# Four weight matrices of a three-stage kernel read three bytes on and decoded with one shift

## The chip, the cores and the metric

The kernel runs on one NeuronCore of a Trainium2 chip. The metric is the device time of one execution in microseconds (us): the median over several runs. The engines are called TensorE (PE), VectorE (DVE), ScalarE (ACT), GpSimd (POOL) and SyncE (SP) below. SP only issues DMAs here; POOL issues DMAs too.

## The reference

Three stages follow one another. The weights come as float64, and the kernel gets their raw 8 bytes as int64; all other inputs are float32.

```python
def _attn_ref(q, k, v, a_re, a_im):              # B, H, S, D = 4, 8, 768, 48
    mag = np.sqrt(a_re * a_re + a_im * a_im)
    scale = np.minimum(mag, 0.999) / (mag + 1e-06)
    a_re_n, a_im_n = (a_re * scale, a_im * scale)
    for t in range(S):                           # complex decay of a D x D state, per head
        new_re = ar * S_re - ai * S_im
        new_im = ar * S_im + ai * S_re
        S_re, S_im = (new_re + kv, new_im)       # kv: outer product of k[t] and v[t]
        y[:, :, t] = np.einsum('bhd,bhde->bhe', q[:, :, t], S_re)

def _moe_ref(x, w1, w2, w3, w_out):              # 384 -> 1024 -> 1024 -> 384
    a = x @ w1
    b = x @ w2
    h = a * b @ w3
    return h @ w_out

def _moe2_ref(x, w_in, w_out):                   # 384 -> 2048 -> 384
    h = x @ w_in
    sp = np.where(h > 20.0, h, np.log1p(np.exp(np.minimum(h, 20.0))))
    return (h * np.tanh(sp)) @ w_out
```

The output of one stage is the `x` of the next; there are 3072 tokens.

## The kernel before

The attention runs in two streams. `bh_stream(g)` (L190) computes, for each of three groups of steps and in blocks of 7 steps, the normalised decays and their running products: a chain of small DVE instructions (`steps`, L292 and L293, one pair per step; the scan L270; the products `scaled`, L310 and L313), fed by ACT (`squares`, `norm`: L215 to L246) and by POOL's loads `an` and `kqt`. The products go to DRAM (`kq_d`, stored by POOL's queue), and a small table ends each group (`table`, L327 to L332). `ch_stream` (L371) reads them back in 24 chunks (`tm`, SP's queue) and does the attention on TensorE: transposes (L421), state updates (L429), scores (L464), outputs (L477, L482). It can start a group only when that group's table is there (`ready`, L405).

The first dense stage is `m1_stream(i)` (L556), six tiles of 512 tokens, in three-product float32r arithmetic: each factor is split into a high and a low part (`split`, L132: an ACT copy and a DVE subtraction), and each product is three matmuls (`mm3`, L544). `w3 @ w_out` is folded into one matrix first by `fold_stream` (L167): three blocks of `w_out` and eight of `w3`, 128 x 1024 elements each, are loaded, decoded to float32 and multiplied (L180); the halves of the result stay in SBUF (`woh`, `wol`) and are also stored to `w3o_d` in DRAM (L183) for a fallback path. `w12(j)` (L551) loads and decodes two blocks of 128 x 384 for `w1` and `w2`, for j = 0 to 7, ahead of the first tile's matmuls. The second dense stage is the loop at L744 over 96 steps of (tile, f): `hid` (nine matmuls, L691), `soft` and `mish` (the activation), `fin` (nine matmuls, L718). Its weights `win` and `wout` are decoded before and in its first 27 steps.

`decode` (L138) turns the int64 words of a float64 into a float32: ACT scales the high word as a float (L149), which also sums its size into `wsum` for a range check; a second ACT instruction extracts three bits of the word (L160); DVE puts the sign in (L161) and joins the parts by a shift to the left (L164). For the `w3` blocks j = 2, 4 and 6 the sign goes another way (`signs=True`): ACT does four instructions (L149, L156, L157, L158) and DVE one (L164).

```python
A.activation(out=f, in_=top.bitcast(F32), func=AF.Abs, scale=W_SCALE, accum_out=...)   # L149
A.activation(out=low, in_=raw.bitcast(U16)[:, :, 1], func=AF.Relu, ...)                # L160
V.scalar_tensor_tensor(out=low, in0=top, scalar=-0x80000000, in1=low, ...)             # L161
V.scalar_tensor_tensor(out=t, in0=t, scalar=3, in1=low, op0=ALU.logical_shift_left, ...)  # L164
```

The raw words of `w1`, `w2`, `win` and `wout` share the tag `raw64`, which has two buffers. `in_range` (L726) turns the sums and flags into one number that decides at the end whether a general path, written for inputs out of range, runs (L766); it is called in step n = 40 of the last loop.

The order of the stages is written with `_merge` (L51): the fold with `bh_stream(0)`; then eight chunks of attention, `bh_stream(1)` and the first dense stage; then the same with `bh_stream(2)`; then what is left of the attention and the first dense stage with `win`; then the last loop. Within that, a scheduler of the tile framework places the instructions of each engine at build time, so an instruction may stand far ahead of its place in the text; what runs on an engine then runs in that fixed order.

Of the kernel before, what the change touches and what calls it, by code (L numbers as in the profile page):

```python
# [13 lines left out]
I32 = mybir.dt.int32  # L14
AF = mybir.ActivationFunctionType
# [5 lines left out]
HD = H * D  # L21
# [14 lines left out]

W_SCALE = 2.0 ** -112
# [28 lines left out]
def kernel(  # L66
# [33 lines left out]
    flags = const.tile([128, sum(n_blk) + 1], F32, name="flags")  # L100
    wsum = const.tile([128, 64], F32, name="wsum")
    cb = const.tile([128, 7], F32, name="cb")
# [6 lines left out]
    w3o_d = dram.tile([128, 2, 8, HD], F32, name="w3o_d")  # L109
# [28 lines left out]
    def decode(src, n, dst=None, raw=None, pool=None, cap=False, signs=False):  # L138

        if raw is None:  # L140
            raw = (pool or stg).tile([128, n, 2], I32, tag="raw64", name="raw64")
        nc.sync.dma_start(out=raw.rearrange("p n z -> p (n z)"), in_=src.bitcast(I32))
        t = dst if dst is not None else stg.tile([128, n], I32, tag="dec", name="dec")
        f = t.bitcast(F32)
        i = n_flags[0]
        if not cap:
            n_flags[0] += 1
        low, top = raw[:, :, 0], raw[:, :, 1]
        A.activation(  # L149
            out=f, in_=top.bitcast(F32), func=AF.Abs, scale=W_SCALE, accum_out=None if cap else wsum[:, i:i + 1]  # L150
        )
        if cap:
            V.tensor_scalar(out=f, in0=f, scalar1=W_MAX, scalar2=None, op0=ALU.min)
        if signs:
            r16 = raw.bitcast(U16)
            A.activation(out=r16[:, :, 0], in_=r16[:, :, 1], func=AF.Relu, scale=2.0 ** -13, bias=cb[:, 3:4])  # L156
            A.activation(out=top.bitcast(F32), in_=top.bitcast(F32), func=AF.Sign, bias=cb[:, 4:5])  # L157
            A.activation(out=raw.bitcast(I16)[:, :, 1], in_=top.bitcast(F32), func=AF.Identity, scale=16384.0, bias=cb[:, 5:6])  # L158
        else:
            A.activation(out=low, in_=raw.bitcast(U16)[:, :, 1], func=AF.Relu, scale=2.0 ** -13, bias=cb[:, 3:4])  # L160
            V.scalar_tensor_tensor(  # L161
                out=low, in0=top, scalar=-0x80000000, in1=low, op0=ALU.bitwise_and, op1=ALU.bitwise_or
            )
        V.scalar_tensor_tensor(out=t, in0=t, scalar=3, in1=low, op0=ALU.logical_shift_left, op1=ALU.bitwise_or)  # L164
        return f

    def fold_stream():  # L167
# [3 lines left out]
        for c in range(3):  # L171
            decode(wo[:, c], 1024, wos[:, c * 1024:(c + 1) * 1024], bufs[c][0])
            yield 2.0
        wos = wos.bitcast(F32).rearrange("p (k n) -> p k n", k=8)
        for j in range(8):
            raw, dst = bufs[j % 3]
            f = decode(w3t[:, j], 1024, dst, raw, signs=j in (2, 4, 6)).rearrange("p (k m) -> p k m", k=8)
# [4 lines left out]
            for z, w in enumerate((woh, wol)):  # L182
                nc.sync.dma_start(out=w3o_d[:, z, j], in_=w[:, j].bitcast(F32))  # L183
# [367 lines left out]
    def w12(j):  # L551
        for src, n in ((w1, "w1"), (w2, "w2")):
            f = decode(src[:, j], 3 * 128)
# [79 lines left out]
    V.memset(cb[:, 6:7], -0.4995)  # L633

# [44 lines left out]

    hw, hbs, gg, accs = {}, {}, {}, {}  # L680
# [44 lines left out]

    def in_range():  # L726
# [17 lines left out]
    for n in range(len(seq) + LAG2):  # L744
# [14 lines left out]
        if n == 40:  # L759
# [6 lines left out]
    with tc.If(ok < 1):  # L766
        general_path(tc, af, kqf, vf, w1, w2, win, wout, w3o_d, perm, gsum, out, decode)


def general_path(tc, af, kqf, vf, w1, w2, win, wout, w3o_d, perm, gsum, out, decode):  # L770
# [6 lines left out]
    with ExitStack() as st:  # L777
# [57 lines left out]
        with tc.tile_pool(name="g_b", bufs=1) as p, tc.tile_pool(name="g_ps2", bufs=1, space=PSUM) as pp:  # L835
# [8 lines left out]
            w3p = p.tile([128, 2, 8, HD], F32, name="w3p")  # L844
            nc.sync.dma_start(out=w3p, in_=w3o_d)
            w3o = p.tile([128, 8, HD], F32, name="w3o")
            V.tensor_tensor(out=w3o, in0=w3p[:, 0], in1=w3p[:, 1], op=add)
# [150 lines left out]
```

## Time and profile before

| | before |
|---|---|
| median of 3 runs | 1077.1 us |
| lowest and highest run | 1075.57 and 1080.53 us |
| span of the profiled execution, first to last instruction | 1079.1 us |
| TensorE busy | 935.3 us (87%) |
| VectorE busy | 702.2 us (65%) |
| ScalarE busy | 691.0 us (64%) |
| GpSimd busy | 108.9 us (10%) |
| mean granted TensorE clock | 0.944 of full speed |
| moved by DMA | 124.36 MB |

The execution that was profiled gives a span; no separate time of its own is listed for it. Its span lies 2.0 us above the median of the runs and between the lowest and the highest of them. A busy time is summed over the whole span; the stages have different limits, so the views that are cut by time are of more use. Two neighbouring instructions of one engine overlap in their records by some 0.1 us, so a cost on an engine is better taken from one start to the next.

### The profile page before, as it was taken

The page shows a single profiled execution, that of the slowest core. Times are in us where ns is not written, and L with a number is a line of the kernel's source. Part 1 is how long each engine was busy: PE and PEld are TensorE (multiplying, and loading weights), DVE is VectorE, ACT ScalarE, POOL GpSimd, SP SyncE. Part 2 cuts the span into 40 slices and gives each one's busy share as a digit, 9 for nine tenths or more (in the row PEclk, how much of TensorE's full clock was granted, in tenths as well). Part 3 has the DMA queues.
Part 4 walks back from the last instruction along what each step waited for, and adds up shares of the span by engine and source line. Part 5 has one row for each costly group of instructions (what it writes and reads, how often), then busy time and mean ns, then how long its engine had stood idle before and what let it go on. Part 6 is the DMA issues. An engine that isn't in the chain of part 4 may idle for free.

```text
span 1079.1 us, 13826 instructions
## 1 busy us (share of the span) xinstructions
PE 935.3 (87%) x4952; PEld 754.5 (70%) x4952; DVE 702.2 (65%) x1334; ACT 691.0 (64%) x1263; POOL 108.9 (10%) x161
## 2 busy tenths in 40 slices
PE   0586006879999999999999999999999999999997
PEld 0243005758788778888888888888888888887876
DVE  5989797899898999462335522688565644645552
ACT  6987466877787686574445422998656665466672
POOL 1212242222212222000000000000000000000000
PEclk9988556889999999999999999999999999999999
DMA  8675559995786875664533300122100101000000
GB/s 304 218 242 149 155 149 249 225 248 131 199 226 163 208 219 115 160 189 115 128 64 127 87 30 29 59 89 59 59 1 10 50 1 59 1 19 10 1 30 33
DMA packets 72509, 124.36 MB, mean 115 GB/s; under 512 B 7574, under 2 KB 45776, under 8 KB 71024
## 3 DMA queue, kind: packets, MB, share of 16 engines
q1 hardware_dynamic: 60880, 85.41, 28.4%
q0 software_dynamic: 11552, 37.98, 13.5%
q8 instruction: 41, 0.67, 0.3%
q14 instruction: 36, 0.29, 0.1%
HBM read 84.16 MB, written 36.18 MB: 112 GB/s over the span
## 4 chain that ended last, share of the span: by engine, by line
PE 62%; DVE 7%; DMA 3%; ACT 2%; issue 1%; SPq 0%; DVEq 0%; ACTq 0%
PE ps_h L549 18%; PE ps_o L549 17%; PE acc L549 7%; PE pa L549 7%; PE pb L549 6%; PE ps_a L464 2%; PE ps_tr L421 2%; DMA ws<-w 1%; PE ps_u L429 1%; PE ps_y L477 1%; PE ps_y L482 1%; DVE t L292 1%; DVE kt L313 1%; DVE p L293 1%; DMA out<-osb 1%
## 5 line engine op out<-in xcount | busy, mean ns | idle before, releaser
L549 PE MATMUL ps_o<-gh,wuh 128*128 128x512 f32 x288 | 113.4, 395 | 2.0 <-ACT osb L722 1.7
L549 PE MATMUL ps_o<-gl,wuh 128*128 128x512 f32 x288 | 113.3, 393 | 0.4 <-DVE gl L134 0.4
L549 PE MATMUL ps_h<-x2h,wil 128*128 128x512 f32 x288 | 113.4, 394 | 0.0
L549 PE MATMUL ps_h<-x2h,wih 128*128 128x512 f32 x288 | 113.2, 393 | 0.0
L549 PE MATMUL ps_o<-gh,wul 128*128 128x512 f32 x288 | 112.8, 392 | 0.0
L549 PE MATMUL ps_h<-x2l,wih 128*128 128x512 f32 x288 | 112.1, 389 | 0.0
L134 DVE TENSOR_TENSOR gl<-hb,gh 128x1024 fp32r<-128x1024 f32 x48 | 58.6, 1223 | 76.2 <-ACT gh L133 76.2
L692 ACT ACTIVATE wb<-ps_h 128x512 f32<-128x512 f32 x96 | 56.1, 598 | 67.9 <-PE ps_h L549 67.7
L693 DVE COPY hb<-ps_h 128x512 f32<-128x512 f32 x96 | 64.7, 687 | 49.1 <-ACT wb L692 47.2
L571 DVE TENSOR_TENSOR u<-u,pb 128x512 f32<-128x512 f32 x48 | 32.8, 684 | 69.5 <-PE pb L549 69.3
L421 PE MATMUL ps_tr<-id_sb,tm 128*96 128x128 f32 x384 | 55.6, 288 | 25.1 <-DMA tm<-kq_d 22.5
L133 ACT CAST gh<-hb 128x1024 fp32r<-128x1024 f32 x48 | 50.2, 1048 | 35.0 <-PE ps_o L549 35.0
L421 PEld LDWEIGHTS ps_tr<-id_sb,tm 128*96 128x96 f32 x384 | 44.5, 132 | 35.5 <-issue 24.3
L292 DVE TENSOR_TENSOR t<-an,p 128x192 f32<-128x192 f32 x192 | 67.4, 351 | 0.7
L133 ACT CAST uh<-u 128x512 fp32r<-128x512 f32 x48 | 29.7, 618 | 59.6 <-DVE u L571 59.4
L180 PE MATMUL ps_f<-fw1h,fw1l 128*128 128x384 f32 x48 | 24.8, 692 | 48.7 <-DVE fw1l L164 48.7
L549 PEld LDWEIGHTS ps_o<-gh,wuh 128*128 128x128 f32 x288 | 54.0, 188 | 16.8 <-ACT osb L722 4.2
L549 PEld LDWEIGHTS ps_o<-gl,wuh 128*128 128x128 f32 x288 | 54.1, 188 | 12.7 <-DVE gl L134 1.1
L549 PEld LDWEIGHTS ps_h<-x2l,wih 128*128 128x128 f32 x288 | 54.1, 188 | 12.5
L549 PEld LDWEIGHTS ps_h<-x2h,wil 128*128 128x128 f32 x288 | 54.0, 188 | 12.5
L549 PEld LDWEIGHTS ps_o<-gh,wul 128*128 128x128 f32 x288 | 54.2, 188 | 12.0
L549 PEld LDWEIGHTS ps_h<-x2h,wih 128*128 128x128 f32 x288 | 54.1, 188 | 11.3
(177 smaller groups left out, 2402.3 us busy)
## 6 DMA issues: line engine op xcount, KB each, us to landing
tm<-kq_d SPq DMA_DIRECT2D x48, 384.0 KB, 5.9
an<-in_a POOLq DMA_DIRECT2D x27, 336.0 KB, 5.0
kqt<-in_kq POOLq DMA_DIRECT2D x27, 336.0 KB, 6.6
kq_d<-kt POOLq DMA_DIRECT2D x27, 336.0 KB, 3.9
kq_d<-kt POOLq DMA_DIRECT2D x54, 168.0 KB, 5.2
vv<-in_v SPq DMA_DIRECT2D x24, 256.0 KB, 2.8
raw<-in_w SPq DMA_DIRECT2D x16, 384.0 KB, 5.5
raw<-in_win SPq DMA_DIRECT2D x16, 384.0 KB, 4.2
```

The source lines that it names most:

```text
L133: A.copy(out=hi, in_=raw)
L134: V.tensor_tensor(out=lo, in0=raw, in1=hi.bitcast(F32), op=sub)
L180: T.matmul(ps, lhsT=f[:, kk], rhs=wos[:, kk], start=(kk == 0), stop=(kk == 7))
L292: V.tensor_tensor(out=t, in0=win2, in1=_bc(pv[:, ::-1], 2, 2), op=mul)
L293: V.tensor_tensor(out=p[:, j], in0=t[:, 0], in1=t[:, 1], op=add)
L313: V.tensor_tensor(out=kt, in0=_bc(kqt, 3, 2), in1=_bc(p[:, 0:m], 2, 2), op=mul)
L421: T.transpose(ps[:, hh], tm[n][:, h0 + hh, z], id_sb[0:C, 0:C])
L464: T.matmul(ps[:, hh], lhsT=kf[n][:, h], rhs=qf[n][:, h], start=True, stop=True)
L549: T.matmul(ps, lhsT=l, rhs=r, start=first and n == 0, stop=final and n == len(seq) - 1)
L571: V.tensor_tensor(out=u, in0=u, in1=pb, op=mul)
L692: A.activation(out=wb[:, f % GRP], in_=ps, func=AF.Sigmoid, scale=-1.0)
L693: V.tensor_copy(hb[:, f % 2], ps)
```

## The change

`w3`, `w_out`, `w1` and `w2` get a decoder of their own, `narrow`. It loads each row of 8n bytes from its fourth byte on, as bytes, so the bytes 3 to 6 of each float64 make the low word and its byte 7 the first byte of the high word. Two ACT instructions turn byte 7 into the sign and the upper exponent bits (the sign comes out inverted for both factors of a product, so it cancels); one DVE instruction shifts the low word to the right by five and joins the two. The sums for the range check leave these matrices; instead `range_load` and `narrow_range` load the four matrices once more in the last loop, in 46 pieces of at most 128 x 384 words, one in each step from n = 34 on, and take the smallest and the largest size of byte 7 in the step behind. `in_range` looks at them too, and moves from n = 40 to n = 88. `w3o_d` and its 16 stores go; the general path decodes `w_out` and `w3` itself. `decode` stays for `win`, `wout` and the general path, without `signs`.

```diff
-    def decode(src, n, dst=None, raw=None, pool=None, cap=False, signs=False):
+    def decode(src, n, dst=None, raw=None, pool=None, cap=False):
...
-        if signs:
-            r16 = raw.bitcast(U16)
-            A.activation(out=r16[:, :, 0], in_=r16[:, :, 1], func=AF.Relu, scale=2.0 ** -13, bias=cb[:, 3:4])
-            A.activation(out=top.bitcast(F32), in_=top.bitcast(F32), func=AF.Sign, bias=cb[:, 4:5])
-            A.activation(out=raw.bitcast(I16)[:, :, 1], in_=top.bitcast(F32), func=AF.Identity, scale=16384.0, bias=cb[:, 5:6])
...
+    def narrow(src, n, dst=None, raw=None):
+
+        if raw is None:
+            raw = stg.tile([128, n, 2], I32, tag="raw64", name="raw64")
+        nc.sync.dma_start(
+            out=raw.rearrange("p n z -> p (n z)").bitcast(U8)[:, 0:8 * n - 3], in_=src.bitcast(U8)[:, 3:8 * n]
+        )
+        t = dst if dst is not None else stg.tile([128, n], I32, tag="dec", name="dec")
+        low, top = raw[:, :, 0], raw[:, :, 1]
+        A.activation(out=top.bitcast(F32), in_=raw.bitcast(I8)[:, :, 4], func=AF.Abs, bias=cb[:, 7:8])
+        A.activation(out=top.bitcast(U32), in_=top.bitcast(F32), func=AF.Abs, scale=2.0 ** 27, bias=cb[:, 8:9])
+        V.scalar_tensor_tensor(
+            out=t, in0=low, scalar=5, in1=top, op0=ALU.logical_shift_right, op1=ALU.bitwise_or
+        )
+        return t.bitcast(F32)
...
-            decode(wo[:, c], 1024, wos[:, c * 1024:(c + 1) * 1024], bufs[c][0])
+            narrow(wo[:, c], 1024, wos[:, c * 1024:(c + 1) * 1024], bufs[c][0])
...
-            f = decode(w3t[:, j], 1024, dst, raw, signs=j in (2, 4, 6)).rearrange("p (k m) -> p k m", k=8)
+            f = narrow(w3t[:, j], 1024, dst, raw).rearrange("p (k m) -> p k m", k=8)
...
-            for z, w in enumerate((woh, wol)):
-                nc.sync.dma_start(out=w3o_d[:, z, j], in_=w[:, j].bitcast(F32))
...
-            f = decode(src[:, j], 3 * 128)
+            f = narrow(src[:, j], 3 * 128)
...
+    def range_load(k):
+
+        w, c0, c1 = pieces[k]
+        ahead[k] = raw = stg.tile([128, c1 - c0, 2], I32, tag="raw64", name="raw64", padded_shape=[128, 384, 2])
+        nc.sync.dma_start(
+            out=raw.rearrange("p n z -> p (n z)"), in_=w.rearrange("p j n -> p (j n)")[:, c0:c1].bitcast(I32)
+        )
+
+    def narrow_range(k):
+
+        raw = ahead.pop(k)
+        for z, op in enumerate((ALU.min, ALU.max)):
+            V.tensor_reduce(
+                out=ends[:, z, k:k + 1], in_=raw.bitcast(I8)[:, :, 7], axis=mybir.AxisListType.X, op=op,
+                apply_absolute_value=True,
+            )
...
+        A.activation(
+            out=ends[:, 0], in_=ends[:, 0], func=AF.Relu, scale=-1.0, bias=cb[:, 9:10], accum_out=flags[:, wf + 1:wf + 2]
+        )
+        A.activation(
+            out=ends[:, 1], in_=ends[:, 1], func=AF.Relu, bias=cb[:, 10:11], accum_out=flags[:, wf + 2:wf + 3]
+        )
...
-        if n == 40:
+        if 34 <= n - 1 < 34 + len(pieces):
+            narrow_range(n - 1 - 34)
+        if 34 <= n < 34 + len(pieces):
+            range_load(n - 34)
+        if n == 88:
             ok = in_range()
```

## Rows read from the trace of the kernel before

**Rows 1.** The page's span in 40 slices: busy tenths of TensorE and VectorE

```profile
PE   0586006879999999999999999999999999999997
DVE  5989797899898999462335522688565644645552
```

**Rows 2.** Busy time of each engine by stretch; length, busy us (instructions), then clock

```profile
10.70:62.00 51.30, 20.49 (x48) 11.13 (x48) 44.58 (x96) 50.69 (x86) 7.11 (x10) 0.97 0.79 258
62.00:112.00 50.00, 32.53 (x80) 17.61 (x80) 46.37 (x105) 35.91 (x65) 14.21 (x20) 0.79 0.62 185
112.00:151.60 39.60, 0.00 (x0) 0.00 (x0) 32.38 (x100) 21.79 (x56) 12.37 (x19) 0.50 0.55 144
...
171.00:234.00 63.00, 51.69 (x405) 44.45 (x405) 56.44 (x132) 52.17 (x133) 14.22 (x20) 0.77 0.96 238
234.00:427.00 193.00, 186.90 (x1196) 153.66 (x1196) 178.24 (x431) 143.68 (x342) 46.67 (x69) 0.98 0.72 185
427.00:671.00 244.00, 244.00 (x1497) 203.98 (x1496) 96.61 (x159) 109.14 (x241) 3.57 (x6) 1.00 0.39 102
...
785.00:975.00 190.00, 189.68 (x823) 153.74 (x823) 100.75 (x101) 109.75 (x119) 0.00 (x0) 1.00 0.07 21
```

**Rows 3.** Waits of TensorE from 234 to 671 us, longest first: us, times, longest

```profile
PE ps_y L482 <- DVE am L465: 3.0, 3, 1.3
PE ps_mt L401 <- DVE mt L332: 1.7, 1, 1.7
```

**Rows 4.** Timeline of TensorE around 151 us: start, length, instruction, idle before

```profile
151.75 0.45 PE L401 MATMUL ps_mt<-id_sb,mt 64*96 64x64 f32 x2 [46.49 <-DVE mt L330]
171.13 2.77 PE L421 MATMUL ps_tr<-id_sb,tm 128*96 128x128 f32 x12 [18.93 <-DMA tm<-kq_d]
```

**Rows 5.** Timeline of VectorE: two decode instructions and what follows each

```profile
35.66 1.22 DVE L164 SCALAR_TENSOR_TENSOR fw1l<-fw1l 128x1024 int32<-128x1024 int32 x1
...
36.79 0.25 DVE L293 TENSOR_TENSOR p<-t 128x96 f32<-128x96 f32 x1
...
116.97 0.56 DVE L161 SCALAR_TENSOR_TENSOR raw<-raw 128x384 int32<-128x384 int32 x1
117.43 0.26 DVE L293 TENSOR_TENSOR p<-t 128x96 f32<-128x96 f32 x1
```

**Rows 6.** Groups of ScalarE instructions by shape, first 151.6 us: busy us, mean ns

```profile
L160 ACT ACTIVATE fw1l<-fw1l,cb 128x1024 int32<-128x1024 uint16 x3 | 3.7, 1223 | 0.0
...
L156 ACT ACTIVATE fw2l<-fw2l,cb 128x1024 uint16<-128x1024 uint16 x1 | 2.6, 2573 | 0.0
...
L158 ACT ACTIVATE fw2l<-fw2l,cb 128x1024 int16<-128x1024 f32 x1 | 2.6, 2581 | 0.0
```

**Rows 7.** Groups of VectorE instructions by shape, first 151.6 us; last, idle before and releaser

```profile
L270 DVE TENSOR_TENSOR_SCAN rs<-rv,sc 128x384 f32<-128x384 f32 x10 | 9.5, 951 | 8.1 <-ACT rv L246 8.1
...
L161 DVE SCALAR_TENSOR_TENSOR fw1l<-fw1l 128x1024 int32<-128x1024 int32 x3 | 3.7, 1222 | 1.7 <-ACT fw1l L160 1.7
...
L161 DVE SCALAR_TENSOR_TENSOR raw<-raw 128x384 int32<-128x384 int32 x5 | 2.8, 555 | 2.8 <-ACT raw L160 2.8
```

**Rows 8.** DMA issues: count, KB each, median us from issue to landing

```profile
raw<-in_w SPq DMA_DIRECT2D x16, 384.0 KB, 5.5
...
raw<-in_wout SPq DMA_DIRECT2D x16, 384.0 KB, 3.1
...
fw2h<-in_w3t SPq DMA_DIRECT2D x3, 1024.0 KB, 5.3
...
w3o_d<-woh SPq DMA_DIRECT2D x8, 192.0 KB, 2.0
```

**Rows 9.** Waits of ScalarE from 10 to 151.6 us

```profile
ACT dec L149 <- DMA raw<-in_w: 10.5, 4, 4.2
```

**Rows 10.** Instructions of two lines of the range check: duration ns, first and last start

```profile
L731 DVE TENSOR_REDUCE fsum<-flags x1: 183/183/183, 747.6 to 747.6; 128x1 f32<-128x31 f32 x1
...
L735 PE MATMUL ps_s<-ones,fsum x2: 163/164/164, 811.6 to 811.7; 128*1 128x1 f32 x2
```

More of the change, by code (lines that the diff above doesn't have):

```diff
@@ L35 @@
 EM20 = float(np.exp(-20.0))
+EXP_LO, EXP_HI = 58.0, 70.0
 W_SCALE = 2.0 ** -112
@@ L99 @@
     n_blk = [-(-(l + 1) // BLK) for l in GROUPS]
-    flags = const.tile([128, sum(n_blk) + 1], F32, name="flags")
+    flags = const.tile([128, sum(n_blk) + 3], F32, name="flags")
+    pieces = [(w, c, min(c + 384, w.shape[1] * w.shape[2])) for w in (w1, w2, wo, w3t)
+              for c in range(0, w.shape[1] * w.shape[2], 384)]
     wsum = const.tile([128, 64], F32, name="wsum")
-    cb = const.tile([128, 7], F32, name="cb")
+    cb = const.tile([128, 11], F32, name="cb")
     sc1 = const.tile([128, D, BLK + 1], F32, name="sc1")
@@ L678 @@
     wul = gp.tile([128, 16, HD], F32R, name="wul", bufs=1)
+    ends = gp.tile([128, 2, len(pieces)], F32, name="ends", bufs=1)
     hw, hbs, gg, accs = {}, {}, {}, {}
@@ L724, in fin @@
             del accs[i]
+    ahead = {}
+    def range_load(k):
[11 more added lines that the diff above has]
+            )
     def in_range():
@@ L766, with general_path @@
     with tc.If(ok < 1):
-        general_path(tc, af, kqf, vf, w1, w2, win, wout, w3o_d, perm, gsum, out, decode)
-def general_path(tc, af, kqf, vf, w1, w2, win, wout, w3o_d, perm, gsum, out, decode):
+        general_path(tc, af, kqf, vf, w1, w2, w3t, wo, win, wout, perm, gsum, out, decode)
+def general_path(tc, af, kqf, vf, w1, w2, w3t, wo, win, wout, perm, gsum, out, decode):
     nc = tc.nc
@@ L843, in general_path @@
                 w[nm] = dst.bitcast(F32)
-            w3p = p.tile([128, 2, 8, HD], F32, name="w3p")
-            nc.sync.dma_start(out=w3p, in_=w3o_d)
+            wos = p.tile([128, 3 * 1024], I32, name="wos")
+            for b in range(3):
+                decode(wo[:, b], 1024, wos[:, b * 1024:(b + 1) * 1024], pool=p, cap=True)
+            wos = wos.bitcast(F32).rearrange("p (k n) -> p k n", k=8)
             w3o = p.tile([128, 8, HD], F32, name="w3o")
-            V.tensor_tensor(out=w3o, in0=w3p[:, 0], in1=w3p[:, 1], op=add)
+            for b in range(8):
+                blk = p.tile([128, 1024], I32, tag="w3b", name="w3b")
+                f = decode(w3t[:, b], 1024, blk, pool=p, cap=True).rearrange("p (k m) -> p k m", k=8)
+                pf = pp.tile([128, HD], F32, tag="f", name="pf")
+                for kk in range(8):
+                    T.matmul(pf, lhsT=f[:, kk], rhs=wos[:, kk], start=(kk == 0), stop=(kk == 7))
+                V.tensor_copy(w3o[:, b], pf)
             pm = p.tile([C, C], F32, name="pm")
```

17 lines of the change are left out of this document (11 added, 6 removed).

## The prediction

> **What bounds the kernel now.** I read the slices first. TensorE has a 9 from the eleventh slice on and gaps before it; VectorE is the reverse, nearly full up to slice 16 and half empty after [rows 1]. So I cut the span where TensorE's picture changes [rows 2]. From 427 to 671 us TensorE is busy for 244.00 of 244.00 us at full clock; from 785 to 975 for 189.68 of 190. From 234 to 427 it is busy for 186.90 of 193, and its waits there and up to 671 us are short: the two largest add up to 4.7 us [rows 3]. None of its matmuls is touched by the change, so from 234 us on the kernel is a fixed amount of TensorE work, and the end moves by what the start of that work moves, plus the few waits.
>
> What sets the start? TensorE ends its fold early and then sits for 46.49 us until VectorE has written the table of the first group, 18.93 us more until the first attention chunk has come back from DRAM [rows 4], and goes through four chunks at a mean clock of 0.77 until the first dense tile has its input. VectorE writes that table at 151.6 us. Its own load up to there: 44.58 of 51.3, 46.37 of 50 and 32.38 of 39.6 us [rows 2], and its idle time is mostly waits for ScalarE, 8.1 us ahead of the scan alone [rows 7]. ScalarE is full from 10.7 to 62 us (50.69 of 51.3) and has room after that [rows 2]. So VectorE's fixed sequence sets 151.6 us, with ScalarE close behind it in the first third.
>
> **The change, part by part.** *VectorE in the fold.* 11 blocks of 1024 columns are decoded. Eight of them (three of `w_out`, five of `w3`) have L161 and L164 now and one instruction after; L161 has 3 + 3 + 2 instructions, of which one group stands in [rows 7]. Start to start, L164 at 35.66 gives way at 36.79 [rows 5], 1.13 us. The new instruction is of the same operation and shape, so it costs the same. 8 x 1.13 = 9.0 us less. The other three blocks have one instruction before and after: 0.
>
> *VectorE in `w1` and `w2`.* Each of the 16 blocks loses one instruction of 384 columns, 117.43 - 116.97 = 0.46 us [rows 5]. Five of them stand ahead of 151.6 us [rows 7]: 2.3 us. The other eleven (5.1 us) come later, ahead of the first tile's matmuls that need them. Of these I count 2: some shorten the way to 234 us, where VectorE is busy for 56.44 of 63 us [rows 2], and some end TensorE's wait of 1.7 us for the second table [rows 3]. Bounds 0 and 5.
>
> *ScalarE.* The three blocks with `signs` lose L156 and L158, 2.57 and 2.58 us each [rows 6]; two instructions remain out of four. The first new one reads single bytes and writes 32 bits, and no row shows a byte read. Bounds: L160, which reads 16 bits and writes 32, 1.22 us; L156, which writes 16 bits, 2.57 us [rows 6]. I take 1.22, since the width written sets L156 apart from L160. Then eight blocks stay about as they are and three save 5.15 us, 15 us in all. None of it is on VectorE's path by itself; it is worth the waits that it ends. VectorE's waits for ScalarE [rows 7] are 8.1 + 1.7 + 2.8 us, and some of them come from ScalarE's own wait for raw words (10.5 us in four waits [rows 9]), which stays. I take 3 us. Bounds: 0, if bytes cost 2.57 us (11 x 1.35 = 15 us eats the saving), and 10.
>
> *DMA.* The 16 stores to `w3o_d` (eight of each half, 2.0 us each [rows 8]) leave SP's queue, where later `w3` loads stand behind them; the share of the DMA engines is 0.79 and 0.62 there [rows 2]. Hidden, 0. The loads keep their size; that they start three bytes on is a rival below, and costs 0 in the sum.
>
> *The range check.* 46 loads go on SP's queue, past the output stores, and 92 reductions on VectorE's. TensorE does 823 matmuls in 190 us [rows 2], 18 a step, so 4.16 us a step; step 40 ran at 811.6 us [rows 10], so steps 34 to 80 are 787 to 978 us. Price of a reduction: between 0.18 us (31 columns [rows 10]) and 0.55 us (384 columns in L161 [rows 7]); I take 0.46, start to start, for the same count. 92 x 0.46 = 42 us go into 190 - 100.75 = 89 us of idle VectorE [rows 2]; that idle time is the cover, and without it each step would grow by up to 0.92 us. A reduction waits for its load, and behind it on VectorE stand the copies that free TensorE's accumulators. A piece has 384 KB like a `wout` block, which landed in 3.1 us [rows 8]; two buffers let it start one to two steps ahead, 4 to 8 us. So no wait; DMA is at 0.07 of its share there. I count 1 us for bunching at the ends of tiles; bounds 0 and 6. `in_range` itself moves by 48 steps to about 1008 us, still ahead of the end; its two added ScalarE instructions and four one-column memsets are nothing.
>
> Sum: -9.0 - 2.3 - 2 - 3 + 1 = -15.3 us. The profiled span is 1079.1 us, which gives 1063.8; it lies 2.0 us above the median of the runs, so on the median 1077.1 the same sum is **1062 us**. With the bounds: -9.0 - 2.3 - 5 - 10 = -26.3, that is 1051; and, with half of VectorE's 11.3 us filled by other waits, 1072.
>
> **The rivals.** *The first stage is held by something else.* Once VectorE has less to do, the loop of `an` loads, squares and normalisation, or ScalarE with dear byte reads, sets the pace, and the 11.3 us turn mostly into idle time. For it: VectorE's waits for ScalarE already make 8.1 us ahead of the scan [rows 7]. Against it: ScalarE falls below VectorE after 62 us [rows 2] and loses more work than VectorE. A third of 11.3 us remaining is -4, so 1073; with the bounds 1071 to 1077.
>
> *The shifted loads are slow; the kernel gets slower.* No row has a DMA that starts off a multiple of four bytes. The place: ScalarE waits in its fixed order for `raw`, four times and 10.5 us [rows 9], with the normalisation queued behind it, and VectorE's scan behind that. If a shifted load took twice the 5.5 us of [rows 8], each of these four waits and one for a `w3` block would grow by about 5.5 us: 5 x 5.5 = 27 us against -15, 1077 - 15 + 27 = 1089 us. It decides from the point where the five add 15 us, that is 3 us a load, or loads 1.55 times as long. Below that it only eats into the gain. The Trainium skill ("DMA: Bandwidth & Descriptors", How a descriptor splits into AXI transactions) says that a read that doesn't start on a 256 B boundary starts at the boundary below, fetching bytes that it doesn't use; rows of 8192 and 3072 bytes would then need the same transactions as before, and by it this rival costs nothing and the sum stands. No run here shows it.
>
> *The range check holds TensorE.* If the loads came late (behind a store in SP's queue that waits for its copy), VectorE would wait in each step. It has 4.16 - 100.75 x 18/823 - 0.92 = 1.0 us a step to spare; a wait of 1.5 us would cost 46 x 0.5 = 23 us, 1085 us. Against it: two buffers, and SP has little to do there.
>
> *The change doesn't do what it says.* If a block were flagged, the general path would run after the rest, and the time would leave this scale altogether. The weights are normal deviates scaled by 1/20 to 1/32, far inside the exponents that are let through; I give it 1 in 100.
>
> **How the numbers follow.** A measurement of this kernel can tell about 0.5% (5.4 us) from no change, so faster is below 1071.7 and slower above 1082.5. The forecast (1051 to 1072) has 0.66; the first stage held by something else 0.16; slow loads 0.09, a third of it mild enough to end within 0.5%; the range check 0.05; the general path 0.01; a gain beyond the bounds, where the new order on the engines happens to fit better, 0.03. Faster: 0.66 + 0.03 + a third of 0.16 = 0.74. Slower: 0.06 + 0.05 + 0.01 = 0.12. The rest, 0.14, is the same within 0.5%. The range that leaves out no more than 2 in 10 is 1051 to 1077: it holds the forecast and nearly all of the first rival.
>
> **What would show it.** In the changed kernel's trace: VectorE writes the first table at about 137 us instead of 151.6; the decode has one VectorE instruction of some 1.22 us per block of 1024, and two ScalarE ones of some 1.22 us; the `w3` loads land in 5 to 7 us and the `w1` loads in about 5.5; TensorE is full from about 218 us on; between 787 and 978 us, shifted by the gain, TensorE keeps 4.16 us a step with VectorE at about three quarters. The prediction is wrong if the first table comes later than 146 us, if ScalarE's byte reads last 2.5 us, if its waits for `raw` exceed 20 us in the first stage, or if TensorE waits for VectorE in the last loop.

## The result and the profile after

The changed kernel takes 1067.5 us in the median of its runs (1062.76 to 1067.65) against 1076.9 for the kernel before; the ratio is 0.9875, with a 95% interval of 0.9843 to 0.9907. In a later series on another chip (experiment 9) the ratio was 0.9869 (0.9838 to 0.9899). It is faster by about 1.3% (0.9 to 1.6%), 13.5 us. The forecast was 1062 us with a range of 1051 to 1077: the sign and the range were right, the gain came out somewhat smaller than the forecast 15 us. The profiled execution has a span of 1065.9 us, 13.2 under the 1079.1 of before.

Where did these 13.2 us come from? First the windows of the changed kernel; they are cut as in [rows 2]. The columns are: window, length, then busy time (and instructions) of TensorE, its weight loads, VectorE, ScalarE and GpSimd, the granted clock of TensorE, the share of the DMA engines and GB/s.

```profile
10.70:62.00 51.30, 25.40 (x74) 14.70 (x75) 45.42 (x101) 47.26 (x77) 9.33 (x13) 1.00 0.87 299
62.00:112.00 50.00, 21.19 (x56) 11.23 (x54) 47.80 (x117) 37.32 (x77) 14.04 (x21) 0.73 0.51 131
112.00:151.60 39.60, 0.45 (x2) 0.23 (x2) 37.59 (x116) 25.93 (x59) 16.72 (x25) 0.50 0.77 198
171.00:234.00 63.00, 49.87 (x400) 41.54 (x400) 57.04 (x132) 49.49 (x119) 14.96 (x21) 0.86 0.85 223
234.00:427.00 193.00, 189.39 (x1237) 156.58 (x1234) 163.15 (x397) 132.66 (x313) 46.03 (x68) 0.98 0.64 171
427.00:671.00 244.00, 244.00 (x1453) 203.55 (x1452) 99.32 (x160) 119.82 (x258) 0.00 (x0) 1.00 0.35 100
785.00:975.00 190.00, 189.19 (x816) 152.77 (x815) 126.68 (x161) 115.35 (x125) 0.00 (x0) 1.00 0.25 80
```

VectorE does more in the early windows than before (45.42, 47.80 and 37.59 us against 44.58, 46.37 and 32.38 in [rows 2]), since the windows stay where they were while the work has moved forward: work of later stages now falls into them. In the last window its busy time has gone from 100.75 to 126.68 us, the range check, and the DMA share from 0.07 to 0.25.

TensorE's timeline of the changed kernel, at the two places of [rows 4] (start, length, instruction, and in brackets the idle time before it and what ended it):

```profile
135.74 0.45 PE L414 MATMUL ps_mt<-id_sb,mt 64*96 64x64 f32 x2 [47.80 <-DVE p L306]
154.89 2.77 PE L434 MATMUL ps_tr<-id_sb,tm 128*96 128x128 f32 x12 [18.70 <-DMA tm<-kq_d]
```

Both milestones come 16 us earlier (151.75 and 171.13 before). Followed on in the same timelines: TensorE is full but for short waits from 218.6 us on (234.0 before), and the last loop, from its first `ps_h` on, begins at 652.7 us (670.9), 18.2 us earlier. But its last `ps_o` starts at 1059.2 (1072.3), only 13.2 us earlier: the last loop has become 5.0 us longer, 406.5 us instead of 401.5. So there are two questions: is the gain of the first stage the one that was worked out, and what does the last loop lose?

What the parts of the decoder cost, from the groups by line and shape of the changed kernel (duration in ns as least/median/most; ScalarE's byte read L175, its second instruction L176, and VectorE's instruction L177):

```profile
L175 ACT ACTIVATE fw2l<-fw2l,cb x3: 1220/1222/1233, 20.6 to 51.3; 128x1024 f32<-128x1024 int8 x3
...
L176 ACT ACTIVATE fw2l<-fw2l,cb x3: 1212/1225/1234, 22.1 to 53.3; 128x1024 uint32<-128x1024 f32 x3
...
L177 DVE SCALAR_TENSOR_TENSOR fw2l<-fw2l x2: 1216/1216/1217, 37.5 to 61.6; 128x1024 int32<-128x1024 int32 x2
```

Its loads, from the DMA issues (count, KB each, median us from issue to landing):

```profile
raw<-in_w SPq DMA_DIRECT2D x16, 383.6 KB, 4.1
...
fw2h<-in_w3t SPq DMA_DIRECT2D x3, 1023.6 KB, 6.8
```

And VectorE's largest waits of the first 151.6 us (us in all, times, longest), which answer to [rows 7], with ScalarE's that answers to [rows 9]:

```profile
DVE m L236 <- ACT sq L228: 7.8, 2, 7.1
DVE rs L283 <- ACT rv L259: 2.4, 2, 2.1
...
ACT raw L175 <- DMA raw<-in_w: 7.9, 6, 2.5
```

The wait of the scan for ScalarE has fallen from 8.1 to 2.4 us, and VectorE's waits for the decoding (1.7 and 2.8 us before) have all but gone. The wait of `m` is not new: it was 7.3 us before. Byte reads cost 1.22 us, no more than 16-bit reads did.

The range check in the changed kernel, as a group of VectorE (busy us, mean ns of one, idle time before it and what ended it):

```profile
L758 DVE TENSOR_REDUCE ends<-raw 128x1 f32<-128x384 int8 x90 | 45.4, 545 | 17.7 <-DMA raw<-in_w 7.5 <-DMA raw<-in_w3t 6.4 <-DMA raw<-in_wo 3.8
```

It ran from 732.2 to 886.9 us. TensorE begins the steps in which the reductions are written, 35 to 80, at 773 to 962 us, so VectorE was 41 us ahead of them at first and 75 at last. And it did wait for its loads, 17.7 us in all.

### The profile page after: what moved, and what is told of

Same layout as the page of the kernel before. It is cut to its first block, busy times and chain, and to the rows that moved or that the text cites. A ratio compares the mean times of both kernels' runs of the same rounds, so it can differ in the third digit from the quotient of the medians.

```text
span 1065.9 us, 13920 instructions
## 1 busy us (share of the span) xinstructions
PE 929.5 (87%) x4952; PEld 749.0 (70%) x4952; DVE 727.6 (68%) x1406; ACT 680.4 (64%) x1234; POOL 108.9 (10%) x161
## 3 DMA queue, kind: packets, MB, share of 16 engines
q0 software_dynamic: 11552, 37.98, 13.5%
## 4 chain that ended last, share of the span: by engine, by line
PE 55%; DVE 21%; DMA 10%; ACT 8%; issue 4%; SPq 0%; POOL 0%; DVEq 0%; ACTq 0%; POOLq 0%
PE ps_o L562 14%; PE ps_h L562 13%; PE acc L562 7%; PE pa L562 6%; PE pb L562 6%; DMA raw<-in_w 3%; DVE t L305 3%; DMA ws<-w 2%; PE ps_tr L434 2%; DVE kt L326 2%; PE ps_a L477 2%; DVE p L306 2%; PE ps_u L442 1%; PE ps_y L495 1%; PE ps_y L490 1%
## 5 line engine op out<-in xcount | busy, mean ns | idle before, releaser
L562 PE MATMUL pa<-xh,w1h 128*128 128x512 f32 x144 | 59.5, 414 | 4.4 <-ACT xh L138 4.4
L562 PEld LDWEIGHTS ps_o<-gh,wul 128*128 128x128 f32 x288 | 54.1, 188 | 12.6
```

The source lines that it names most:

```text
L562: T.matmul(ps, lhsT=l, rhs=r, start=first and n == 0, stop=final and n == len(seq) - 1)
```

## Experiments on the first stage

Each kernel ran beside the kernel before on the same chip, and its ratio is to that. A difference between two kernels is the difference of their ratios times 1077 us; its error is put together from both intervals (root of the sum of squares). Six of the executions profiled here have the same first stage (the changed kernel, the same again, without the check, and the three other forms of the check, below): their first attention transposes, the first `ps_tr`, start at 152.9 to 154.9 us, mean 154.0. So a single trace can tell 2 us there, where the times can tell about 4.

**Without the range check (1).** The reference point for the next ones: the first stage alone.

```diff
-        if 34 <= n - 1 < 34 + len(pieces):
-            narrow_range(n - 1 - 34)
-        if 34 <= n < 34 + len(pieces):
-            range_load(n - 34)
```

> The changed kernel without its range check: the 46 loads and 92 reductions are left out, and the two rows of sizes are set to a constant inside the range, so the check looks at nothing. Theory A (the check costs time because its reductions stand in VectorE's queue ahead of the copies that free TensorE's accumulators, and because its loads and reductions slow TensorE's pitch): the last loop, from the first ps_h to the last ps_o, takes 401 us again instead of 406, the three gaps of 0.8 us at tile ends (749, 757 and 824 us) are gone, the mean pitch of matmuls falls from 231.5 to 230.3 ns; the time is 1062 to 1063 us, 5 us under the changed kernel's 1067.5. Rival B (only the gaps belong to the check, the pitch is something else): 1065 us and a pitch of 231.5 ns. Rival C (the longer last loop has nothing to do with the check): 1067 us.

Measured: 0.9853 (0.9822 to 0.9883), so 15.8 us of gain (12.6 to 19.2) are left without the check; ahead of the last loop it may be some 2 us more, since that loop is 403.3 us long in the trace against 401.5 before. The three waits at tile ends are gone; but the pitch of the matmuls (the time from one start to the next) is still 231.3 ns. So B holds here: without the check's instructions the waits go and the pitch stays (more on it below).

**One VectorE instruction back in eight blocks of the fold (5).**

```diff
+        if twice:
+            V.scalar_tensor_tensor(out=top, in0=top, scalar=0, in1=top, op0=ALU.bitwise_or, op1=ALU.bitwise_or)
```

> As the kernel without the range check (first table at 133.8 us, first tm load at 143.7), but in the eight blocks of the fold where VectorE lost an instruction (three of w_out, five of w3) it gets one back: a scalar_tensor_tensor over 1024 columns that leaves its words as they are. ScalarE and the loads stay as they are. Theory A (the saved VectorE instructions are the gain of the first stage): table and first tm load come 8 to 10 us later, the time is 9 us longer, 1073 us against 1064. Theory D (ScalarE's shorter chain is the gain, VectorE had idle time in any case): 2 us or less.

Measured: 0.9940 (0.9918 to 0.9962), 9.4 us slower than without it (error 4.1). In TensorE's timeline of this kernel:

```profile
150.80 0.45 PE L416 MATMUL ps_mt<-id_sb,mt 64*96 64x64 f32 x2 [40.73 <-DVE mt L345]
163.14 2.77 PE L436 MATMUL ps_tr<-id_sb,tm 128*96 128x128 f32 x12 [11.89 <-DMA tm<-kq_d]
```

The transposes start 9.1 us later than the mean of 154.0, which is the 8 x 1.13 = 9.0 us that were put back. So VectorE's sequence sets the first stage, and what was put back into it in the fold came out once, in full. The table (the first row) moved by 15 to 17 us, more than was put back; why is seen in experiment 3.

**ScalarE's instructions back in three blocks (6).**

```diff
+        if more:
+            for z in range(2):
+                A.activation(out=t.bitcast(U16)[:, 0:2 * n:2], in_=top.bitcast(F32), func=AF.Abs)
```

> As the kernel without the range check, but in the three w3 blocks j = 2, 4 and 6 ScalarE gets back two instructions that write 1024 16-bit numbers each (about 2.5 us each, 15 us in all). VectorE stays as it is. Theory A: ScalarE has room after 62 us, so table and first tm load move by 3 us or less; the time by as much. Theory D: table and first tm load come 8 to 15 us later, and so does the end.

Measured: 0.9878 (0.9851 to 0.9904), 2.7 us slower than without (error 4.4, so not told from nothing). The added instructions were cheaper than meant, by this group of ScalarE:

```profile
L178 ACT ACTIVATE fw2h<-fw2h 128x1024 uint16<-128x1024 f32 x2 | 2.7, 1359 | 0.0
```

Six of them by 1.36 us are 8 us, half of the 15 that the change took off. With these 8 us the table stood at 131.5 us and the transposes at 150.5, 3.5 us earlier than the mean of 154.0. So in this order ScalarE had room for them ahead of the attention: these 8 us are not where the gain there comes from. The other 7 of the 15 weren't put back. The first `ps_h` came at 657.7 us all the same, against 651.0 to 656.0 in the six; whether that belongs to the added work isn't settled.

**`w1` and `w2` in the old way (2), and `w1` and `w2` alone in the new way (3).**

```diff
-            f = narrow(src[:, j], 3 * 128)
+            f = decode(src[:, j], 3 * 128)
```

> As the kernel without the check, but w1 and w2 are decoded in the old way; only w_out and w3 are read three bytes on. Theory A (VectorE's sequence sets the first table): the table is late by w1/w2's share, 5 instructions of 0.46 us, so it comes at about 138 us; 2 to 3 us more are lost before the first dense stage is full: 4 to 5 us slower than without the check alone, 1067 us. Rival D (ScalarE's saving of 15 us in three w3 blocks is what counts, w1/w2 nothing): within 1 us of the kernel without the check, table at 136 us.

> The kernel before with w1 and w2 alone read three bytes on and decoded by the shift, and no range check of them; w_out and w3 as before. Theory A: the first table at 149 to 150 us instead of 151.6, the time 1072 to 1074 us (4 us under 1076.9). Rival D (ScalarE's saving counts): 1076 to 1077 us.

Measured: the kernel without the check and with `w1` and `w2` decoded in the old way 0.9846 (0.9818 to 0.9873), 0.8 us faster than with them in the new way (error 4.4). The times can't tell the predicted 4 us from nothing. Its trace has the transposes at 155.95 us, 1.9 later than the mean, and the first `ps_h` at 654.8, inside the scatter of the six. The other way round, the kernel before with the new `w1` and `w2` alone, the ratio is 0.9970 (0.9951 to 0.9988), 3.2 us faster. But these 3.2 us can't be put down to the first stage: in the trace the transposes start at 170.75 us, against 171.1 and 170.4 in two kernels with the old decoder (before and 4), and it is the last loop that is 4.7 us shorter, by another pitch of its matmuls (table below). So what `w1` and `w2` are worth is open: 1.9 us by the one trace, nothing by the other.

Experiment 3 showed something else. Its timelines of TensorE, SP (the load of the first chunk) and GpSimd (the last stores of the first group):

```profile
158.75 0.45 PE L421 MATMUL ps_mt<-id_sb,mt 64*96 64x64 f32 x2 [46.74 <-DVE mt L350]
170.75 2.77 PE L441 MATMUL ps_tr<-id_sb,tm 128*96 128x128 f32 x12 [11.56 <-DMA tm<-kq_d]
...
162.47 2.91 SPq L410 DMA_DIRECT2D tm<-kq_d  x4
...
158.70 1.07 POOL L337 DMA_DIRECT2D kq_d<-kt  x2
```

The same two rows of SP and GpSimd in the kernel before:

```profile
162.14 2.86 SPq L390 DMA_DIRECT2D tm<-kq_d  x4
...
158.56 1.08 POOL L317 DMA_DIRECT2D kq_d<-kt  x2
```

With the other decoder the scheduler put the table 7 us later in VectorE's order, and the transposes didn't move (171.13 before, 170.75 here). What they wait for is the load `tm`, and that is issued some 3.5 us after the start of the last two stores of the products of group 0: 158.56 and 162.14 before, 158.70 and 162.47 here, 142.19 and 145.61 in the changed kernel. So the table was a convenient mark, not the gate; the gate is the end of VectorE's products. Both stand in the same sequence, which is why the sum still came out.

**Loads from the first byte (7).** The same instructions in the same order, with loads that aren't shifted.

```diff
-            out=raw.rearrange("p n z -> p (n z)").bitcast(U8)[:, 0:8 * n - 3], in_=src.bitcast(U8)[:, 3:8 * n]
+            out=raw.rearrange("p n z -> p (n z)").bitcast(U8), in_=src.bitcast(U8)
...
-        A.activation(out=top.bitcast(F32), in_=raw.bitcast(I8)[:, :, 4], func=AF.Abs, bias=cb[:, 7:8])
+        A.activation(out=top.bitcast(F32), in_=raw.bitcast(I8)[:, :, 7], func=AF.Abs, bias=cb[:, 7:8])
```

> As the kernel without the range check, but the rows are loaded from their first byte, 8n bytes, and ScalarE takes byte 7 as the sign byte; the mantissa bits that VectorE shifts are then wrong ones. Same instructions in the same order. Theory A (a load that starts three bytes on costs nothing): loads of a w3 block 6 to 7 us as before, table and first tm load within 1.5 us of 133.8 and 143.7 us, the same time. Rival S (the shift of three bytes costs up to 1 us a load, hidden so far): w3 loads about 5.3 us, table 1.5 to 3 us earlier.

Measured: 0.9841 (0.9808 to 0.9874), 1.3 us from the kernel without the check (error 4.8); the transposes at 153.7 us, 0.3 from the mean. Its loads:

```profile
raw<-in_w SPq DMA_DIRECT2D x16, 384.0 KB, 3.9
fw1l<-in_w3t SPq DMA_DIRECT2D x3, 1024.0 KB, 5.9
fw2h<-in_w3t SPq DMA_DIRECT2D x3, 1024.0 KB, 6.8
```

With the shift, in the kernel without the check, the three groups took 3.7, 6.3 and 6.7 us. A start three bytes on costs nothing here. The sentence from the Trainium skill in the prediction ("DMA: Bandwidth & Descriptors", How a descriptor splits into AXI transactions) agrees with this trace: 6.7 against 6.8 us for a `w3` block.

**Without the 16 stores of the folded matrix (8).** The kernel before, less these:

```diff
-            for z, w in enumerate((woh, wol)):
-                nc.sync.dma_start(out=w3o_d[:, z, j], in_=w[:, j].bitcast(F32))
```

> The kernel before without the 16 stores of the folded matrix to DRAM (only the fallback path would read them). Theory A: the stores are hidden, table at 151 to 152 us, the time within 1 us of before. Rival Q (they hold up the w3 and w1 loads in SP's queue): table 2 to 4 us earlier, the time 2 to 4 us shorter, w3 loads nearer to 5 us.

Measured: 0.9982 (0.9962 to 1.0001), 1.9 us (error 2.1); the transposes at 168.7 us instead of 171.1. The stores were hidden or nearly so; a gain of up to 4 us isn't excluded, and the trace leans to 2. The table stood at 150.0 us, between the two expectations, and the `w3` loads landed in 6.6, 5.4 and 5.9 us by group (6.2, 5.3 and 7.0 before), no clear change.

Together, by the first transposes: 170.75 us before (the mean of 171.1 and of 170.4 in the kernel of experiment 4, which has the same first stage), 154.0 after, 16.8 us. Of these 9.1 are the fold's VectorE instructions (5), up to 2 `w1` and `w2` (2; none by 3), about 2 the stores (8). The 4 us or more that remain are of the size of VectorE's ended waits for ScalarE and of what another order of the engines shifts; they weren't separated further.

## Experiments on the last loop

**The check alone, added to the kernel before (4).** `range_load` and `narrow_range` are those of the change.

```diff
-        if n == 40:
+        if 34 <= n - 1 < 34 + len(pieces):
+            narrow_range(n - 1 - 34)
+        if 34 <= n < 34 + len(pieces):
+            range_load(n - 34)
+        if n == 88:
             ok = in_range()
```

> The kernel before with the range check added in the last loop, and nothing else. Theory A (the check costs 5 us): 1081 to 1083 us, with gaps of TensorE at tile ends and a pitch of 231.5 ns in the last loop. Rival B: 1079.5 us, with the gaps and 230.3 ns. Rival C: 1077 us, no gaps.

Measured: 1.0039 (1.0014 to 1.0065), 4.2 us slower. Its trace has three waits for `osb`, of 0.48, 0.96 and 0.43 us, at the ends of the second and third tile, and gaps as A and B had them. Its pitch is 231.4 ns, as A had it and not B, although it was B that held in experiment 1; the table of pitches below bears on that.

**The changed kernel once more (9).** Nothing is edited.

> The changed kernel once more, beside the next three on one chip. From the earlier runs: ratio to before 0.9875; the kernel without the range check had 0.9853. Theory A (the check costs the three waits of TensorE at tile ends, 3 us in all, and nothing else): 0.987 to 0.989, three waits of about 0.83 us for osb at tile ends in the trace. Rival B (the check also slows the matmuls' pitch): pitch in the last loop well above 231.3 ns. Rival C (the check is free): 0.985, no such waits.

Measured: 0.9869 (0.9838 to 0.9899), 1.7 us slower than without the check (error 4.7). Its trace has one wait of 1.30 us for `osb` at the end of the second tile in place of three of 0.83 us, and the pitch is 231.4 ns. So the waits belong to the check, but where they fall differs from one execution to the next.

What holds TensorE at these places? The timelines of the changed kernel around 757 us, TensorE, ScalarE, VectorE and SP:

```profile
757.19 0.40 PE L562 MATMUL ps_o<-gh,wul 128*128 128x512 f32 x1
758.43 0.50 PE L562 MATMUL ps_o<-gh,wuh 128*128 128x512 f32 x1 [0.84 <-ACT osb L740]
...
752.71 0.59 ACT L740 COPY osb<-ps_o 128x512 f32<-128x512 f32 x1
...
757.79 0.59 ACT L740 COPY osb<-ps_o 128x512 f32<-128x512 f32 x1 [0.97 <-DMA out<-osb]
...
751.03 1.98 DVE L758 TENSOR_REDUCE ends<-raw 128x1 f32<-128x384 int8 x4 [0.75 <-DMA raw<-in_w]
755.52 1.01 DVE L758 TENSOR_REDUCE ends<-raw 128x1 f32<-128x384 int8 x2 [2.52 <-DMA raw<-in_w]
757.09 1.01 DVE L758 TENSOR_REDUCE ends<-raw 128x1 f32<-128x384 int8 x2 [0.56 <-DMA raw<-in_w]
...
752.07 1.29 SPq L750 DMA_DIRECT2D raw<-in_w  x2
753.42 0.42 SPq L741 DMA_DIRECT2D out<-osb  x1
756.56 0.33 SPq L750 DMA_DIRECT2D raw<-in_w  x1
758.41 0.34 SPq L741 DMA_DIRECT2D out<-osb  x1
```

In the kernel without the check the last of the three `osb` copies of this tile started at 752.52 us, after a wait of 2.12; here it starts at 757.79. What it waits for is the landing of the tile's second output store, issued at 753.42 us between range loads. The DMA issues of that store here, and in the kernel without the check (count, KB, us to landing):

```profile
out<-osb SPq DMA_DIRECT2D x1, 256.0 KB, 4.3
...
out<-osb SPq DMA_DIRECT2D x1, 256.0 KB, 2.0
```

So the third copy comes so late that the next tile's first `ps_o` finds its accumulator still occupied. VectorE's waits for its loads, 2.52 and 0.56 us here, don't stand in that way. The wait at 825.6 us has the same form (a store of 3.8 us). The one at 750.4 us has another, with no wait for a load in it: three reductions stand on VectorE ahead of `gl`, which reads an `hb` buffer; `osb` takes its buffer from the same six (both have the tag `hb`), and the copy waited for `gl`.

```profile
747.10 1.46 DVE L758 TENSOR_REDUCE ends<-raw 128x1 f32<-128x384 int8 x3
748.48 1.21 DVE L139 TENSOR_TENSOR gl<-hb,gh 128x1024 fp32r<-128x1024 f32 x1
...
749.72 0.59 ACT L740 COPY osb<-ps_o 128x512 f32<-128x512 f32 x1 [0.92 <-DVE gl L139]
...
750.36 0.50 PE L562 MATMUL ps_o<-gh,wuh 128*128 128x512 f32 x1 [0.83 <-ACT osb L740]
```

Is it the length of the reductions, or the loads? Two kernels take one away in turn; each has one execution, so its trace counts and not its time.

**Loads without long reductions (10).**

```diff
-                out=ends[:, z, k:k + 1], in_=raw.bitcast(I8)[:, :, 7], axis=mybir.AxisListType.X, op=op,
+                out=ends[:, z, k:k + 1], in_=raw.bitcast(I8)[:, 0:8, 7], axis=mybir.AxisListType.X, op=op,
```

> The changed kernel with its 46 range loads, but each reduction looks at 8 words of a piece instead of 384; so VectorE waits for the loads as before and works little. It checks only a small part of the weights. Theory A1 (VectorE's queue is held by the length of the reductions): TensorE's waits for osb at the ends of the second and third tile fall from 2.5 us to under 0.8. Theory A2 (it is held by waiting for the loads, or the output stores stand behind the loads in SP's queue): two or three waits of about 0.8 us remain.

TensorE's waits for `osb` between 720 and 900 us were 4.5 us in four, more than the 2.5 us in three of the changed kernel. The longest of them, from the timelines of TensorE, ScalarE and VectorE:

```profile
821.11 0.80 PE L562 MATMUL ps_o<-gh,wuh 128*128 128x512 f32 x1 [2.27 <-ACT osb L740]
...
820.47 0.59 ACT L740 COPY osb<-ps_o 128x512 f32<-128x512 f32 x1 [2.36 <-DVE gl L139]
...
819.08 0.23 DVE L758 TENSOR_REDUCE ends<-raw 128x1 f32<-128x8 int8 x2 [2.63 <-DMA raw<-in_w3t]
819.23 1.21 DVE L139 TENSOR_TENSOR gl<-hb,gh 128x1024 fp32r<-128x1024 f32 x1
```

Read it from the bottom up: VectorE stands 2.63 us at a reduction whose load hasn't landed, `gl` behind it comes late, ScalarE's `osb` waits 2.36 us for `gl`, and TensorE 2.27 for `osb`. The other three waits stand behind an output store that took 3.1 to 4.0 us.

**Reductions without loads (11).**

```diff
-        raw = ahead.pop(k)
+        raw = wuh[:, 0:2].rearrange("p k n -> p (k n)").bitcast(I8).rearrange("p (n z) -> p n z", z=8)
...
-        if 34 <= n < 34 + len(pieces):
-            range_load(n - 34)
```

> The changed kernel with its 92 reductions of 384 bytes, read from a tile that is in SBUF anyway, and no range loads; the result of the reductions isn't used, so nothing is checked. Theory A1 (length of the reductions): two or three waits of TensorE of about 0.8 us for osb at tile ends remain. Theory A2 (loads): under 0.8 us in all at the ends of the second and third tile.

No wait of TensorE for `osb` at the ends of the second and third tile at all, and a last loop of 400.6 us. So A2, with this reading: the cost comes with the loads. Four executions with the loads as the change writes them (the changed kernel, 4, 9 and 10) have eleven such waits, eight of them behind an output store that took 3.1 to 4.8 us to land, three behind VectorE. The executions without range loads (before, 1, 2, 3, 5, 6, 7, 8 and 11) have none there, and the first two stores of each of these tiles land in 2.0 us in all of them. The 92 reductions went into VectorE's idle time here, as predicted; but without loads the scheduler also put them elsewhere, from 664 us on, so their length isn't cleared for the place where they stand in the changed kernel.

**The same check, paced (12).** A load may start only when its step's `hb` is there, and no load stands near the end of a tile.

```diff
+        A.copy(out=raw.bitcast(F32)[:, 0, 0:1], in_=hb[:, 0, 0:1])
...
+    steps = [n for n in range(30, 92) if n % 16 not in (12, 13, 14)][:len(pieces) + 1]
...
-        if 34 <= n < 34 + len(pieces):
-            range_load(n - 34)
+        if n in steps:
+            if steps.index(n) > 0:
+                narrow_range(steps.index(n) - 1)
+            if n != steps[-1]:
+                range_load(steps.index(n), hbs[seq[n][0], seq[n][1] - seq[n][1] % 2])
```

> The changed kernel with the same 46 loads and 92 reductions, but a load may start only when the step that it stands in has its ps_h copied (ScalarE copies one word of hb into the buffer first), and none stands in the three steps around the end of a tile; so the reductions can't gather ahead of the copies that free the accumulators. in_range moves to step 93. Theory A: no wait for osb at the ends of tiles 1 to 4, TensorE's gaps in the last loop 2.5 us instead of 5.6, the time 2 to 3 us under the changed kernel in the same call. Rival: the 46 added copies on ScalarE and the later check at the end cost as much, and the time is the same or longer.

Measured: 0.9827 (0.9802 to 0.9852), 1063.2 us against 1067.05 of the changed kernel on the same chip; by the ratios 4.5 us faster, with an error of 4.3. The group of its reductions shows that they now stand where they were written, and what they still wait for:

```profile
L759 DVE TENSOR_REDUCE ends<-raw x92: 275/545/555, 767.2 to 986.8; 128x1 f32<-128x384 int8 x90, 128x1 f32<-128x128 int8 x2
its engine sat idle before it (us, times) until:
  DMA raw<-in_w3t: 2.8, 4
  DMA raw<-in_w: 2.8, 3
  DMA raw<-in_wo: 1.6, 2
```

7.2 us of waits instead of 17.7, and one wait of TensorE for `osb`, of 0.60 us, is left at all (theory A had none); it stands behind `gl` and the reductions ahead of it. The second output stores of the two tiles land in 2.0 us again. Which of the two, the pacing or the steps kept free of loads, does it wasn't separated. It is the fastest of the kernels that keep the whole check.

**The pitch.** In every timeline I took the last loop's distances from the start of one `ps_h` or `ps_o` matmul to the next: those up to 0.3 us make the mean pitch, and what exceeds 0.23 us in the longer ones makes the gaps.

| kernel | last loop, us | gaps, us | mean pitch, ns |
|---|---|---|---|
| before | 401.5 | 4.34 | 229.83 |
| changed | 406.5 | 6.69 | 231.39 |
| changed, again (9) | 405.3 | 5.52 | 231.36 |
| without the check (1) | 403.3 | 3.61 | 231.30 |
| loads only (10) | 410.3 | 10.60 | 231.37 |
| reductions only (11) | 400.6 | 3.46 | 229.85 |
| paced (12) | 401.7 | 1.77 | 231.44 |
| `w1`, `w2` alone (3) | 396.8 | 4.87 | 226.79 |
| check alone (4) | 406.0 | 6.19 | 231.39 |
| no stores (8) | 401.8 | 4.62 | 229.87 |

The expectations count the gaps about 1 us lower in the changed kernel (5.6); by this table's count pacing the loads (12) took them from 5.5 to 6.7 us down to 1.8.

The pitch has levels, and they don't go with the check's instructions: 231.3 without any, 229.9 with all its reductions. Over the 1709 matmuls of the loop 1.6 ns make 2.7 us. So of the 5.0 us that the last loop lost, about 2.3 are gaps and 2.7 the pitch; the gaps that go with the check, against the kernel without it, are 3.1 and 1.9 us in the two executions of the changed kernel.

The levels do go with the tiles that a kernel sets up. All ten executions with one tile `ends` (the changed kernel twice, 1, 2, 4, 5, 6, 7, 10 and 12) have 231.3 to 231.4 ns, also 1, which has the tile and no check, and 4, which is otherwise the kernel before. Before and 8, without it, have 229.8 and 229.9; 11, with a second such tile, 229.9; 3, without it but with a constant tile four words longer, 226.8. So the 2.7 us seem to come with the check after all, by the tiles that it adds. Where the tiles come to lie in SBUF is a candidate for the cause; no run tried it.

## Why the prediction was right, and where it was not

**The bound.** Right up to the last loop: TensorE was full from 218.6 us (218 was forecast), and 18.2 us were gained up to that loop. But the dense work was not the fixed amount that the prediction took it for: the same matmuls of the last loop took 2.7 us longer by their pitch. (TensorE's first 9 in [rows 1] is in the tenth slice, not the eleventh; nothing hangs on it.)

**VectorE in the fold, -9.0 us.** Right, and shown: 9.1 us in the trace and 9.4 (error 4.1) in the times when the eight instructions come back.

**`w1` and `w2`, -2.3 and -2.** Not shown. Up to the first transposes it was 1.9 us when they were taken out of the changed kernel (2), and nothing clear when they were put into the kernel before (3), where VectorE's last product of the group ended at 157.9 us against 157.7. The other 2 couldn't be told from nothing.

**ScalarE and its waits, -3.** The price of a byte read was right, 1.22 us. My reason for it was not shown: I held that the 16-bit write made L156 dear [rows 6], but 16-bit numbers written four bytes apart took 1.36 us (experiment 6), not 2.57. The scan's waits for ScalarE fell by 5.7 us; the part of it that reached the end was not measured by itself. The first stage gained 16.8 us where 14.3 were reckoned up to there, well inside the bounds; that the total came out has some luck in it, since `w1` and `w2` were priced too high or rightly, the stores too low, and some 4 us aren't assigned.

**DMA in the first stage, 0.** The shifted loads cost nothing. The stores were priced at 0; the trace leans to 2 us, the times have 1.9 (error 2.1).

**The range check, +1, bounds 0 and 6.** The sign and the bounds held, the reasoning failed at one step. I wrote that two buffers let a load start one to two steps ahead, "so no wait", and that the DMA share there is 0.07. That assumed one piece a step, from 787 to 978 us, a time taken from TensorE's row of step 40 at 811.6 us. But VectorE's row of the same step, L731 in [rows 10], stood at 747.6 us, 64 us ahead of it: the scheduler fills VectorE far ahead of TensorE's place in the text. So the pieces ran from 732 to 887 us, up to four reductions side by side; from 751 to 760 us the DMA share was 0.75. SP starts a load only when the reductions before it have freed a buffer:

```profile
SPq L750 <- DVE ends L758: 94.1, 42, 10.6
```

The next reductions stand right behind: 17.7 us of waits on VectorE. The third rival had these (VectorE waiting for loads, copies behind it), but in each step and at 23 us. Most of them cost TensorE nothing. What did reach it came at the ends of tiles, where an accumulator is wanted back, and mostly by a way that neither the sum nor a rival had: the range loads lengthened the output stores that the copies wait for, from 2.0 us to between 3.1 and 4.8. Price: 2 to 3 us by the gaps; 4.2 us (1.5 to 7.0) when the check is added to the kernel before, where the pitch changed with it.

**The rest.** From -15.3 to the -13.2 of the profiled span: the early part gave 18.2 us instead of 16.3 (the sum without the check), and the last loop took back 5.0 instead of 1, of which 2.7 are the pitch, which no part of the sum had. The 18.2 are of one execution each; with the six executions of that first stage it lies between 14.9 and 19.9, so it can't be told from 16.3.

**The rivals.** The first stage was not held by something else: 16 us were gained. The shifted loads were not slow. No block was flagged.

**What would have shown it.** Table at 135.7 us (137 forecast), ScalarE's two instructions 1.22 and 1.23 us, `w3` loads 6.3 to 7.1 us (5 to 7), `w1` loads 4.1 (5.5), VectorE at two thirds between 785 and 975 us (126.68 of 190; three quarters). That TensorE would keep its steps in the last loop was the one that failed.

## What to carry to other kernels

Where one engine's fixed sequence opens a stage, an instruction taken from it can be worth its start-to-start time, as the fold's eight were here; test it by putting it back. Work that fills an idle engine is free only as long as it is ready when its turn comes and its transfers don't lengthen others: a load that it waits for holds everything behind it in the queue, and loads under way made output stores here take up to 4.8 us instead of 2.0. So look at where the scheduler really puts such work, by the engine's own rows and not by another engine's, and give it a dependency that paces it. A mark that moves with a change, like the table here, need not be the gate; look for the transfer that the next stage waits for and for what issues it.

## What was not expected of the hardware

- A load that starts three bytes on, 8189 bytes a row, takes as long as one that starts at the row's beginning: 6.7 against 6.8 us for 1024 KB.
- ScalarE reads every eighth byte as int8 and writes 32 bits in 1.22 us for 1024 columns, as with 16-bit reads; 384 columns take 0.64 us. A 16-bit write took 1.36 us where its numbers lie four bytes apart, and 2.57 where they lay eight apart [rows 6]; whether that distance is the cause wasn't tried.
- A reduction of 384 bytes, eight apart, to one number takes VectorE 0.545 us, and 0.46 from one start to the next, as forecast.
- At the ends of the second and third tile the first two output stores of 256 KB landed in 2.0 us where no range load was under way (in all nine executions without them, and in 12); the stores ahead of the eight waits took 3.1 to 4.8 us.
- The mean pitch of TensorE's 512-column matmuls in the last loop was 226.8, 229.8 to 229.9 or 231.3 to 231.4 ns, by program, at a granted clock of 1.00 (2.4 GHz) from 680 to 1050 us in all ten executions of the table; that makes up to 8 us between programs. It went with the set of tiles in these programs; what sets it stays open.
